# Two of the three ScalarE steps of a float64-to-float32 conversion write float32 words in place of bf16 half-words

## The chip, the cores and the metric
The kernel runs on one core of a Trainium2 chip (trn2). The metric is the device time of one launch in microseconds (us). TensorE (PE) does the matmuls, ScalarE (ACT) activations and copies, VectorE (DVE) and GpSimd (POOL) elementwise work, and SyncE (SP) issues most of the DMAs.

## The reference, cut to what matters
Attention with a soft cap (4 batches, 12 heads, 448 positions, 64 per head) is followed by two mixers: a token mix and a channel MLP, then a Fourier mix, a normalization and a second channel MLP:

```python
scores = cap * np.tanh(scores / cap)          # attention, softmax over the last axis
h  = np.maximum(xt @ w_tok1, 0.0) @ w_tok2    # first mixer: tokens 448 -> 256 -> 448
h2 = np.maximum(u @ w_ch1, 0.0) @ w_ch2       # channels 768 -> 1536 -> 768
mixed = np.real(np.fft.fft(np.fft.fft(x, axis=1), axis=2))
ch = np.maximum(un @ w_ch1, 0.0) @ w_ch2      # second mixer: 768 -> 3072 -> 768
```

The factors 1/sqrt(n) make the weights of both mixers float64. They lie in device memory as 8-byte words, and the kernel turns them into float32 itself: this conversion is what the change touches.

## The kernel before, in words
**Stages.** In the trace the heads and the token mixing fill about the first 300 us. Then comes the first channel MLP (to about 600 us), then the Fourier mix for one pair of batches beside the MLP (600 to 750), the second channel MLP for one half (750 to 1050) and for the other, in seven products after Strassen, up to the end at 1469 us. Each float32 product is made as three matmuls of a high and a low part (`mm3`, lines 301 to 304).

**Conversion.** `convert` (line 351) turns a piece of up to 128 rows by 768 float64 values into float32. A DMA on SP's queue loads the piece with its first three bytes cut off (lines 364 to 368), so that each value fills two 32-bit words of the `raw` tile: word 0 holds bytes 3 to 6, and the lowest byte of word 1 holds byte 7, with sign and upper exponent. The other three bytes of word 1 hold the three lowest bytes of the next value, which nothing uses. Three ScalarE instructions (line 330, called in lines 370 to 373) turn byte 7 into the sign and the top of the exponent of a float32: the first reads int8, the second and third read what the one before wrote, and the third writes word 1 as int32. A DVE instruction (line 374) shifts word 0 and joins both into the result, either in place or in a tile `y`. Every operand of these steps steps by 8 bytes from value to value.

**Who calls it.** `tok_first` and `tok_second` convert four narrow pieces; `piece` (line 398) converts a piece that is needed soon, and splits it into high and low parts `wh`, `wl`; `ahead` (line 1271) converts weights of the second MLP early, and puts them back into device memory (`put`, line 415) from the tile `y`. For its first eight pieces it also splits and puts both parts.

**Order.** The order on every engine is fixed when the kernel is built. A planner (`Plan.run`) picks operations by ready time, cost and due-time offsets. A copy on ScalarE is charged `fixed["A"] + n / 1150` us, whatever types it reads and writes (line 321), and the DMA of a piece cols/350 us. The engines run their queues in that order; at run time only semaphores hold them. There are two `raw` tiles, and a third from the end of the heads on, and two `y` tiles.

Of the kernel before, what the change touches and what calls it, by code (L numbers as in the profile page):

```python
# [9 lines left out]
F32 = mybir.dt.float32  # L10
# [4 lines left out]
BF16 = mybir.dt.bfloat16  # L15
# [249 lines left out]
def kernel(  # L265
# [48 lines left out]
    def v(n):  # L314
        return {"V": fixed["V"] + n / 960}
# [13 lines left out]
    def copy(n, out, src, reads, writes, func=AF.Copy, **kw):  # L329
        pl.op(a(n), lambda e: A.activation(out=out(), in_=src(), func=func, **kw), reads, writes)  # L330
# [14 lines left out]
    def raw_slot():  # L345
        return pl.slot("raw", lambda sp: (sp or raw_p).tile([128, TW, 2], I32, tag="raw", name="raw"))

    def flat(raw, dt=I32):
        return raw().rearrange("p a b -> p (a b)").bitcast(dt)

    def convert(src, rows, cols, x=None):
        raw = raw_slot()
        top = (raw, "top")

        def word(i):
            return raw()[:rows, :cols, i]

        def part(dt, n):
            return lambda: raw().bitcast(dt)[:rows, :cols, n]

        def value(dt=F32):
            return x().bitcast(dt)[:rows, :cols] if x else flat(raw, dt)[:rows, :cols]

        pl.op(
            {"SP": cols / 350}, lambda e: nc.sync.dma_start(
                out=flat(raw, I8)[:rows, :8 * cols - 3], in_=src.bitcast(I8)[:, 3:]
            ), [], [raw], lag=2.15,
        )
        step = part(BF16, 2)
        copy(cols, step, part(I8, 4), [raw], [top], AF.Relu, bias=72.0)  # L370
        copy(cols, step, step, [raw], [top], AF.Prelu, scale=-1.0, bias=16.0, alpha=KINK)
        copy(cols, lambda: word(1), step, [raw], [top], AF.Prelu,
             scale=-FIELD / KINK, bias=-112.0 * FIELD, alpha=KINK)
        pl.op(v(cols), lambda e: V.scalar_tensor_tensor(
            out=value(I32), in0=word(0), scalar=5, in1=word(1), op0=ALU.logical_shift_right, op1=ALU.bitwise_or,
        ), [raw, top], [x or raw])
        return value, x or raw
# [20 lines left out]
    def piece(src, x=None, k=None, engs=vp):  # L398
        w, ws = w_slot()
        value, key = convert(src, 128, DM, x)  # L400
        halves(DM, value, part(w, 0), part(w, 1), [key, w], ws[1:], engs)
        if k is not None:
            put(value, [key], k)
        return w, ws
# [42 lines left out]
    def phase_ab(heads, mixer, banks_a, banks_b):  # L447
# [29 lines left out]
        def tok_first():  # L477
            for i in range(2):
                value, key = convert(tok1[i], CP, 2 * DTOK)
                split_in(2 * DTOK, value, key, lambda i=i: rows2(w1h, i), lambda i=i: rows2(w1l, i), "w1", i)  # L480

        def tok_second():
            for i in range(2):
                value, key = convert(tok2[i], 128, S)
                split_in(S, value, key, lambda i=i: w2h[:, i, :], lambda i=i: w2l[:, i, :], "w2", i)
# [1470 lines left out]
```

## Time and profile before

| | us |
|---|---|
| median of 3 runs | 1470.07 (1463.83 to 1480.21) |
| the profiled execution | 1470.81 |
| its span, first to last instruction | 1469.0 |
| PE busy | 1377.9 |
| DVE busy | 1035.2 |
| ACT busy | 912.1 |
| POOL busy | 307.4 |

The busy time of an engine is the sum over its instructions. The chain of waits follows the last instruction back to what released it, step by step. The mean granted TensorE clock was 0.976 of full speed.

### The profile page before, as it was taken

Reading aid. Unit: us, or ns where it says so; the run is one execution under the profiler, and the core shown is the slowest. Engines: PE = TensorE matmul, PEld = TensorE weight load, DVE = VectorE, ACT = ScalarE, POOL = GpSimd, SP = SyncE. Lnnn points to the kernel's source line nnn. Section 1 sums busy time; section 2 is a strip of 40 time slices with the busy share of each in tenths; the row PEclk is TensorE's granted clock in tenths of the full one; section 3 lists DMA queues with packets and bytes.
Section 4 is the critical chain, followed back from the end, with each engine's and each line's share of the span. In section 5 each row is a group of like instructions: output and inputs, shape, how many; then the busy total and the mean of one; then the engine's idle time right before and its main releaser. Section 6 shows DMA issues by size and latency. Waiting matters only on the chain.

```text
span 1469.0 us, 18918 instructions
## 1 busy us (share of the span) xinstructions
PE 1377.9 (94%) x7398; PEld 1134.4 (77%) x7398; DVE 1035.2 (70%) x1076; ACT 912.1 (62%) x899; POOL 307.4 (21%) x166
## 2 busy tenths in 40 slices
PE   7899999989989879999998999889989999999997
PEld 2345545589879769899987889878778998999986
DVE  7887888646543445566886888575888778767698
ACT  8977897689899998212329552767722454444542
POOL 3332314100000000000000445221233223222341
PEclk9999999999999989999999999999999999999998
DMA  4222121027767776622436869886729866633332
GB/s 125 80 66 95 55 85 57 8 86 240 262 217 226 218 244 216 188 87 99 149 113 225 277 242 346 306 306 223 244 90 326 303 228 220 228 109 108 99 118 97
DMA packets 83771, 257.53 MB, mean 175 GB/s; under 512 B 9376, under 2 KB 12320, under 8 KB 83682
## 3 DMA queue, kind: packets, MB, share of 16 engines
q1 hardware_dynamic: 82528, 253.70, 52.0%
q0 software_dynamic: 1152, 2.62, 0.7%
q8 instruction: 58, 0.95, 0.3%
q14 instruction: 31, 0.25, 0.0%
q10 hardware_dynamic: 2, 0.00, 0.0%
HBM read 181.47 MB, written 74.81 MB: 174 GB/s over the span
## 4 chain that ended last, share of the span: by engine, by line
PE 58%; ACT 20%; DMA 10%; DVE 7%; issue 4%; SPq 1%; POOL 0%; DVEq 0%; ACTq 0%; POOLq 0%
PE mm L302 15%; PE mm L303 15%; PE mm L304 15%; ACT raw L330 13%; PE sc L519 3%; PE av L587 3%; DMA kept<-raw 3%; DMA raw<-in_m_dram 2%; ACT t L524 2%; ACT t L544 2%; PE mx L714 2%; DMA kept<-y 1%; PE av L603 1%; DMA wl<-kept 1%; DMA raw<-kept 1%
## 5 line engine op out<-in xcount | busy, mean ns | idle before, releaser
L330 ACT ACTIVATE raw<-raw 128x768 bf16<-128x768 int8 (+6 forms) x251 | 372.7, 1509 | 65.3 <-DMA raw<-kept 34.1
L302 PE MATMUL mm<-u,wh 128*128 128x448 f32 x804 | 296.9, 369 | 15.1 <-ACT wh L330 6.7
L303 PE MATMUL mm<-u,wh 128*128 128x448 f32 x828 | 304.6, 368 | 1.8 <-DVE u L333 1.8
L304 PE MATMUL mm<-u,wl 128*128 128x448 f32 x804 | 295.8, 368 | 0.0
L302 PE MATMUL mm<-r,wh 128*128 128x448 f32 x618 | 234.2, 379 | 26.3 <-DVE z L333 12.2
L303 PE MATMUL mm<-r,wh 128*128 128x448 f32 x624 | 235.1, 377 | 10.4 <-DVE r L333 4.8
L333 DVE TENSOR_TENSOR z<-mm,z 128x896 f32<-128x896 f32 (+1 forms) x205 | 203.6, 1011 | 49.3 <-PE mm L304 48.3
L304 PE MATMUL mm<-r,wl 128*128 128x448 f32 x618 | 231.0, 374 | 0.0
L330 ACT ACTIVATE wh<-wl 128x768 fp32r<-128x768 f32 x113 | 95.6, 848 | 163.7 <-DMA wl<-kept 159.7
L302 PEld LDWEIGHTS mm<-u,wh 128*128 128x128 f32 x804 | 152.4, 190 | 30.8 <-ACT wh L330 7.0
L303 PEld LDWEIGHTS mm<-u,wh 128*128 128x128 f32 x828 | 156.7, 189 | 15.1 <-DVE u L333 2.6
L333 POOL TENSOR_TENSOR wl<-wl,wh 128x768 fp32r<-128x768 f32 x37 | 75.1, 2034 | 426.9 <-ACT wh L330 218.3
L304 PEld LDWEIGHTS mm<-u,wl 128*128 128x128 f32 x804 | 152.4, 190 | 13.5 <-DVE wl L333 0.5
L302 PEld LDWEIGHTS mm<-r,wh 128*128 128x128 f32 x618 | 120.1, 194 | 43.6 <-DVE z L333 11.7
L303 PEld LDWEIGHTS mm<-r,wh 128*128 128x128 f32 x624 | 121.4, 195 | 22.9 <-DVE r L1524 5.7
L536 POOL PARTITION_ALL_REDUCE mb<-m x48 | 90.8, 1939 | 182.5 <-DVE m L333 153.4
L304 PEld LDWEIGHTS mm<-r,wl 128*128 128x128 f32 x618 | 119.9, 194 | 10.3
L333 DVE TENSOR_TENSOR wl<-wl,wh 128x768 fp32r<-128x768 f32 x76 | 83.8, 1108 | 50.9 <-ACT wh L330 50.7
L330 ACT ACTIVATE u<-u 128x896 fp32r<-128x896 f32 (+4 forms) x61 | 53.8, 892 | 105.5 <-DVE u L333 78.2
L330 ACT ACTIVATE r<-mm 128x896 fp32r<-128x896 f32 (+5 forms) x81 | 66.9, 831 | 75.9 <-PE mm L304 37.0
L333 DVE TENSOR_TENSOR t<-t,mb 112x1792 f32<-112x1792 f32 x48 | 103.4, 2176 | 6.3 <-POOL mb L536 6.3
L524 ACT ACTIVATE t<-sc,scl 112x896 f32<-112x896 f32 x96 | 92.8, 1012 | 9.0 <-PE sc L519 8.4
(191 smaller groups left out, 2139.7 us busy)
## 6 DMA issues: line engine op xcount, KB each, us to landing
wl<-kept SPq DMA_DIRECT2D x133, 384.0 KB, 3.7
raw<-in_m_dram SPq DMA_DIRECT2D x48, 767.6 KB, 5.0
raw<-kept SPq DMA_DIRECT2D x71, 384.0 KB, 4.6
kept<-raw SPq DMA_DIRECT2D x68, 384.0 KB, 4.8
raw<-in_c_dram SPq DMA_DIRECT2D x24, 767.6 KB, 5.0
kept<-y SPq DMA_DIRECT2D x44, 384.0 KB, 4.0
u<-kept SPq DMA_DIRECT2D x24, 448.0 KB, 6.1
qr<-in_qk_dram SPq DMA_DIRECT2D x23, 448.0 KB, 3.3
```

What stands on the lines that cost most here:

```text
L302: T.matmul(out=dst, lhsT=wh, rhs=xh, start=first, stop=False, skip_group_check=more)
L303: T.matmul(out=dst, lhsT=wh, rhs=xl, start=False, stop=False, skip_group_check=more)
L304: T.matmul(out=dst, lhsT=wl, rhs=xh, start=False, stop=last, skip_group_check=more)
L330: pl.op(a(n), lambda e: A.activation(out=out(), in_=src(), func=func, **kw), reads, writes)
L333: pl.op(engs, lambda e: eng[e].tensor_tensor(out=out(), in0=in0(), in1=in1(), op=op), reads, writes)
L519: T.matmul(out=ps()[:CP, k, :S], lhsT=qr()[d, S + c * CP:S + (c + 1) * CP], rhs=qr()[d, :S], start=True, stop=True)
L524: pl.op(a(W2, 0.06), lambda e, c=c, ps=ps: A.activation(out=tl()[:, c], in_=ps()[:CP, :, :S], func=AF.Tanh, scale=scl[:CP, 0:1]), [ps, tl] ...
L536: pl.op({"P": 1.9}, lambda e, k=k: P.partition_all_reduce(mb()[:, k], mx()[:, k], CP, bass_isa.ReduceOp.max), [mx, mb], [kb], hold=0.75)
L544: pl.op(a(2 * W2, 0.1), lambda e, k=k: A.activation(out=tl()[:, :, k], in_=tl()[:, :, k], func=AF.Exp, scale=cap_sb[:CP, 0:1]), [tl], [ke])
L587: T.matmul(out=ps()[d, :S], lhsT=vv()[:, c, d], rhs=tl()[:, c, hd], start=(c == 0), stop=(c == NCH - 1))
L603: T.matmul(out=ps()[32 * k:32 * k + 32, :S], lhsT=ones[:CP, 0:32].bitcast(F32), rhs=tl()[:, c, hd], start=(c == 0), stop=(c == NCH - 1))
L714: T.matmul(out=ps()[:, :S], lhsT=channels_of(rt()[:, tb, c], kc % NJ), rhs=wt[:, tb, :], start=False, stop=last, skip_group_check=True)
```

## The change
The first and the second ScalarE step of the conversion write, and the second and third read, a float32 in word 1 in place of a bf16 in its lower half. The functions, scales and biases stay, and so do the operations, their number, their tiles and what they are charged in the plan.

```diff
@@ -366,7 +366,7 @@
                 out=flat(raw, I8)[:rows, :8 * cols - 3], in_=src.bitcast(I8)[:, 3:]
             ), [], [raw], lag=2.15,
         )
-        step = part(BF16, 2)
+        step = part(F32, 1)
         copy(cols, step, part(I8, 4), [raw], [top], AF.Relu, bias=72.0)
         copy(cols, step, step, [raw], [top], AF.Prelu, scale=-1.0, bias=16.0, alpha=KINK)
         copy(cols, lambda: word(1), step, [raw], [top], AF.Prelu,
```

`part(BF16, 2)` is half-word 2 of each group of 8 bytes, `part(F32, 1)` is word 1, and `word(1)` is the same place as int32.

## Rows read from the trace of the kernel before

**Rows 1.** Profile page, busy time of each engine, and its share in 40 slices.

```profile
PE 1377.9 (94%) x7398; PEld 1134.4 (77%) x7398; DVE 1035.2 (70%) x1076; ACT 912.1 (62%) x899; POOL 307.4 (21%) x166
ACT  8977897689899998212329552767722454444542
```

**Rows 2.** Windows by stage: from:to, length, busy (instructions), granted clock, DMA share, GB/s.

```profile
0.00:300.00 300.00, 283.57 (x2038) 139.84 (x2039) 236.73 (x223) 244.17 (x259) 92.48 (x55) 0.99 0.25 76
300.00:390.00 90.00, 83.25 (x409) 76.71 (x409) 48.98 (x50) 78.45 (x71) 1.20 (x1) 0.96 0.51 175
390.00:550.00 160.00, 136.21 (x627) 121.69 (x626) 73.28 (x75) 156.89 (x113) 1.85 (x1) 0.94 0.72 230
550.00:600.00 50.00, 49.69 (x238) 45.49 (x237) 25.61 (x27) 38.74 (x30) 4.35 (x5) 0.97 0.65 221
600.00:750.00 150.00, 148.61 (x803) 137.03 (x802) 105.22 (x140) 34.52 (x43) 2.13 (x4) 1.00 0.37 118
750.00:850.00 100.00, 89.71 (x486) 80.32 (x484) 77.45 (x93) 64.73 (x60) 17.44 (x8) 0.97 0.66 228
850.00:1000.00 150.00, 141.06 (x660) 128.31 (x661) 112.64 (x124) 78.33 (x76) 52.57 (x29) 0.95 0.85 295
1000.00:1050.00 50.00, 47.71 (x231) 42.70 (x230) 28.20 (x32) 45.34 (x49) 8.45 (x6) 1.00 0.72 234
1300.00:1350.00 50.00, 50.00 (x248) 46.23 (x247) 33.53 (x33) 22.94 (x27) 14.57 (x7) 1.00 0.36 106
```

**Rows 3.** Chain of waits by line, 390 to 550 us.

```profile
by line: ACT raw L330 71.2%; issue 11.6%; ACT wh L330 4.1%; DMA raw<-in_m_dram 3.9%; ACT r L330 3.0%; PE mm L303 1.4%; DVE r L787 1.3%; DVE raw L374 1.2%; DVE y L374 1.1%; PE mm L304 0.7%; PE mm L302 0.5%; SPq L416 0.2%; DVE wl L333 0.0%; A
```

**Rows 4.** Waits of PE, 390 to 550 us: total us, times, longest.

```profile
PE mm L302 <- ACT r L330: 8.9, 2, 5.3
PE mm L302 <- ACT wh L330: 6.7, 1, 6.7
```

**Rows 5.** ACT's instructions by form, whole span: count, busy us, mean ns, idle before.

```profile
L330 ACT ACTIVATE raw<-raw 128x768 bf16<-128x768 bf16 x72 | 140.5, 1951 | 1.6
L330 ACT ACTIVATE raw<-raw 128x768 bf16<-128x768 int8 x72 | 140.3, 1956 | 26.5 <-DMA raw<-in_m_dram 10.8 <-DMA raw<-in_c_dram 9.5 <-DMA kept<-raw 5.2
L330 ACT ACTIVATE wh<-wl 128x768 fp32r<-128x768 f32 x113 | 95.6, 848 | 163.7 <-DMA wl<-kept 159.7 <-DVE raw L333 3.2
L330 ACT ACTIVATE raw<-raw 128x768 int32<-128x768 bf16 x72 | 65.1, 904 | 1.6
L330 ACT ACTIVATE raw<-raw 112x512 bf16<-112x512 int8 x2 | 2.7, 1358 | 0.0
L330 ACT ACTIVATE raw<-raw 112x512 int32<-112x512 bf16 x2 | 1.4, 688 | 0.0
```

**Rows 6.** DVE's instructions by form, 390 to 550 us.

```profile
L374 DVE SCALAR_TENSOR_TENSOR y<-raw 128x768 int32<-128x768 int32 x21 | 20.7, 984 | 46.3 <-ACT raw L330 46.3
L333 DVE TENSOR_TENSOR wl<-raw,wh 128x768 fp32r<-128x768 f32 x9 | 8.6, 956 | 11.3 <-ACT wh L330 11.3
```

**Rows 7.** ACT's instructions by form, 390 to 550 us.

```profile
L330 ACT ACTIVATE raw<-raw 128x768 bf16<-128x768 int8 x31 | 60.4, 1950 | 1.0 <-DMA raw<-in_c_dram 0.9
L330 ACT ACTIVATE raw<-raw 128x768 bf16<-128x768 bf16 x31 | 60.1, 1940 | 0.8
```

**Rows 8.** DMA issues, 300 to 620 us: count, KB each, us to landing.

```profile
raw<-in_m_dram SPq DMA_DIRECT2D x27, 767.6 KB, 4.9
kept<-y SPq DMA_DIRECT2D x44, 384.0 KB, 4.0
```

**Rows 9.** Chain of waits by line, 300 to 390 us.

```profile
by line: DMA kept<-y 23.6%; ACT raw L330 19.7%; DMA raw<-in_m_dram 11.8%; PE mx L714 6.9%; PE mm L302 5.5%; PE mm L303 5.0%; PE mm L304 4.9%; DVE y L374 4.3%; DVE y L333 3.2%; issue 3.2%; ACT u L330 2.9%; PE mx L710 2.4%; ACT y L330 2.0%; A
```

**Rows 10.** Chain of waits by line, 765 to 830 us, then ACT's forms there.

```profile
by line: ACT raw L330 35.3%; PE mm L302 12.1%; PE mm L304 11.4%; PE mm L303 11.3%; issue 10.4%; DMA raw<-in_m_dram 6.5%; ACT r L330 4.6%; ACT u L330 2.9%; DVE z L333 1.7%; DVE raw L374 1.6%; DVE mm L791 1.6%; PE mm L907 0.9%; ACTq L330 0.1%
...
L330 ACT ACTIVATE raw<-raw 128x768 bf16<-128x768 bf16 x7 | 13.6, 1943 | 0.2
```

## The prediction, made before the changed kernel had run

> **What bounds the kernel now.** I began with the busy times: PE is busy for 94% of the span, ACT for 62%, which by itself would put ACT off the path. The slices say otherwise: ACT's digits stand at 9 in a run of slices in the first half and at 2 to 7 later [rows 1]. So I cut the span into stages. Between 390 and 550 us ACT is busy for 156.89 of 160 us, while PE runs only 627 matmuls; between 1300 and 1350 us, a stretch of nearly the same three-matmul products, PE runs 248 in 50 us at full clock, 0.2016 us each [rows 2]. At that rate the 627 need 126.4 us, so the stage is 33.6 us longer than PE needs. That includes PE's lower clock: the mean granted clock is 0.94 there against 1.00, that is, part of the time at 1.2 GHz in place of 2.4, in a stage in which PE stands waiting. The chain of waits runs through ACT's conversion steps for 71.2% of the stage [rows 3], and PE waits longest for other ACT results, evictions `r` and splits `wh`, that stand behind conversions in ACT's queue [rows 4]. Here ACT sets the time. Elsewhere PE does: 148.61 of 150 us from 600 to 750 us [rows 2].
>
> **The price of one step.** The second and third steps of the conversion read the same bf16 half-words at the same 8-byte distance. The second writes bf16 and takes 1951 ns, the third writes int32 words and takes 904 ns [rows 5]. The first reads int8, writes bf16 and takes 1956 ns. What the two slow ones share and the fast one lacks is the 2-byte output. A contiguous float32 copy of the same size takes 848 ns [rows 5], so 904 is near the floor. After the change the first two steps write 4-byte words where the third writes them now: I take 904 ns for both. Bounds: 848 below, 1956 above (if int8 reading, in the first, or float32 reading at 8 bytes' distance, in the second and third, costs as much as the half-word writes). No ACT row shows such a float32 read; on DVE, line 374 reads 4-byte words at 8 bytes' distance and takes 984 ns, against 956 for a contiguous operation of the same size [rows 6], so I price it at nothing, and put the upper end into a rival.
>
> The saving is 1047 + 1052 = 2099 ns for each 768-wide piece; the rows count 72, so 151 us of ACT's time. The two pieces of 512 columns have 1358 against 688 ns, the same pattern [rows 5].
>
> One page speaks against this. The Trainium skill (ScalarE: Activation LUTs, section What ACT_TABLE_LOAD costs) says an ACTIVATE runs at one element per cycle and lane for every function, float32 and bf16 alike; by its 186 + 0.833 N ns a step of 768 takes an estimated 826 ns whatever the type, and the change would save nothing. The trace disagrees on the steps of today by more than a factor of two.
>
> **Stage by stage.** The plan's costs don't see the type, so every queue keeps its order; no wait, DMA or instruction is added, and nothing is moved past anything. Only durations change, and what follows from them.
>
> *390 to 550 us.* 31 + 31 slow steps [rows 7] shorten by 1.05 us each: 65 us off ACT's 156.89, leaving 92, less than the 126.4 that PE needs. PE becomes the bound, and at most 33.6 us can come back. What is late next is the load of a piece: a `raw` tile is refilled only when the DVE step has released it, 4.9 us to landing [rows 8], then ACT 3 x 0.9, DVE 0.98, about 8.6 us; over three tiles 2.9 us per piece, where PE's need leaves 126.4/31 = 4.1. A `y` tile has 0.98 of DVE and a put of 4.0 us to landing [rows 8], 5 us over two tiles: 2.5. Both fit. But DMA's busy share of 0.72 over 160 us would become 0.91 over 126.4, and between 850 and 1000 us, at 0.85, PE runs 660 matmuls, 133 us of work in 150, so queues crowd there [rows 2]. I take 27 of the 33.6.
>
> *300 to 390 us.* The largest terms of the chain are `kept<-y` (23.6%) and loads (11.8%); ACT's conversions have 19.7% [rows 9]. The puts of the eight pieces that are put three times bound it, and don't get faster. PE is idle for 6.75 us [rows 2]; I take 4 (between 0 and 6.75).
>
> *550 to 600 us.* 238 matmuls need 48.0 of 50 us [rows 2]: 1 us.
>
> *0 to 300 us.* PE is idle for 16.4 us [rows 2], and the few conversions stand between tanh and exp in ACT's queue. I take 4 (0 to 16.4).
>
> *750 to 850 us.* The chain has 35.3% of 65 us in conversions, 23 us, and 7 pieces shorten by 14.7 us [rows 10]; PE is idle for 10.3 [rows 2]. The reductions of the Fourier mix go through DVE as well, so I take 8. *1000 to 1050 us*: ACT is busy for 45.34 us and PE idle for 2.3 [rows 2]; 2. *850 to 1000 us* and after 1050: nothing; DMA or PE sets the pace.
>
> A lead won before 600 us is kept: PE has no slack from 600 to 750 us to lose it in. Sum: 4 + 4 + 27 + 1 + 8 + 2 = 46 us. The profiled execution took 1470.81 us (its span 1469.0 and 1.8 around it), 0.7 from the median of 1470.07, so I forecast **1425 us**.
>
> **The rivals.**
> *DMA takes ACT's place.* If the stage from 390 to 550 us can't go above the share of 0.75 (a little over its 0.72 now), it shrinks only to 160 x 0.72 / 0.75 = 154 us: 6 in place of 27, and the total is 1446. For it: the loads wait for tiles, and faster steps make them come together. Against: 0.85 is held for 150 us at 295 GB/s later [rows 2].
>
> *More comes back.* Waits after 850 us also come from evictions behind late conversions. If all 33.6 come back, and of the 6.75, 16.4, 10.3 and 2.3 some 28, and 8 of the 17 us that 850 to 1000 us lacks, it is 70 us: 1400.
>
> *The type makes no difference.* By the page's rule, as a mechanism of this kernel: the 1951 and 1956 ns come from function or data (Relu and Prelu with a bias), not from output size, and the steps stay so: 1470. Against: the third step is also a Prelu with scale, bias and alpha, on the same bytes, at 904 [rows 5]. The Trainium skill's page on ScalarE, named above, is where this rule stands.
>
> *Slower.* Reading float32 at 8 bytes' distance is slow on ACT. The first step becomes 904, and the second and third take R each; today's three make 4.81 us, so it decides from R = 1.95 up. At R = 2.35 (1.95 and 0.4 more) a piece takes 5.6 us, 0.8 more, and 31 pieces on the ACT-bound chain, with the 7 at 765 us, add 30 us: 1500. Against: DVE's 984 [rows 6], and the third step's 904 for a read of the same pitch.
>
> **How the numbers follow.** Forecast and its surroundings (1410 to 1440) 0.70; DMA instead (1440 to 1456) 0.12; more (1395 to 1410) 0.11; no difference 0.04; slower 0.03. The range reaches from 1400 to 1446: the whole first case, and most of its two neighbours. About 1% (15 us) is what a measurement here can tell from no change; the runs spread by that much. Faster by over 1% (under 1455) needs only a third of the forecast gain: 0.91. Within 1%: the no-difference case and the tail of the DMA case, 0.06. Slower: 0.03.
>
> **What would show it.** In the changed trace: `raw<-raw` float32 steps at about 0.9 us, none near 1.95; ACT's total near 760 us; the chain between 390 and 510 us through PE, with conversions no more its largest term; DMA's share there above 0.8; PE's granted clock near 1.00. I am wrong in the price if either step stays above 1.5 us; wrong in the path if the steps take 0.9 us and the time is above 1446, and then the waits name the `raw` loads or the `kept<-y` puts.

## The result and the profile after

The changed kernel takes 1401.44 us (median of 4 runs, 1397.42 to 1406.28) against 1474.16 for the kernel before beside it: a ratio of 0.9515, 95% interval 0.9448 to 0.9582. In a second comparison the same kernel had 0.9548 (0.9509 to 0.9586). The forecast was 1425 with a range of 1400 to 1446, so the time lies 1.4 us inside the low edge: 73 us were won where the sum had 46.

The price of a step first. ACT's instructions by form, whole span, of the changed kernel (to hold against [rows 5]: count, busy us, mean ns, idle before):

```profile
L330 ACT ACTIVATE raw<-raw 128x768 f32<-128x768 f32 x72 | 65.7, 913 | 1.6
L330 ACT ACTIVATE raw<-raw 128x768 int32<-128x768 f32 x72 | 65.4, 908 | 1.6
L330 ACT ACTIVATE raw<-raw 128x768 f32<-128x768 int8 x72 | 65.0, 906 | 73.5 <-DMA raw<-in_m_dram 36.1 <-DMA raw<-in_c_dram 30.4 <-issue 3.6
```

1951 and 1956 ns became 913 and 906; the third step, 904 before, took 908. Then the page, and the last line as it was before:

```profile
PE 1352.8 (97%) x7398; PEld 1121.7 (80%) x7398; DVE 1037.7 (74%) x1076; ACT 769.4 (55%) x899; POOL 302.8 (22%) x166
...
ACT  8977897676687763123255513657313643444442
...
L330 ACT ACTIVATE raw<-raw 128x768 f32<-128x768 int8 (+6 forms) x251 | 221.3, 891 | 116.7 <-DMA raw<-kept 39.9
```

```profile
L330 ACT ACTIVATE raw<-raw 128x768 bf16<-128x768 int8 (+6 forms) x251 | 372.7, 1509 | 65.3 <-DMA raw<-kept 34.1
```

The run of nines in ACT's slices [rows 1] is gone. The group of ACT instructions from `raw` to `raw`, all conversions and 23 splits, has 221.3 us; before it had 372.7, so 151 us less, about what the price times the count said. ACT as a whole lost 142.7 us (912.1 to 769.4, where the prediction had near 760): busy time counts a stretch once where two instructions overlap, and with idle time between them fewer do.

Where the time came from is best read by cutting the changed trace where PE has issued as many matmuls as at 300, 390, 550, 600, 750, 850, 1000 and 1050 us before. Windows of the changed kernel, cut so (columns as in [rows 2]):

```profile
0.00:290.10 290.10, 279.70 (x2039) 139.51 (x2040) 237.32 (x223) 235.11 (x260) 92.69 (x55) 1.00 0.26 79
290.10:369.90 79.80, 79.80 (x409) 74.50 (x408) 47.64 (x49) 54.87 (x70) 1.16 (x1) 1.00 0.57 190
369.90:499.40 129.50, 127.80 (x626) 117.28 (x625) 73.58 (x76) 97.22 (x114) 1.85 (x1) 1.00 0.85 289
499.40:548.90 49.50, 49.50 (x237) 45.66 (x236) 25.69 (x27) 25.53 (x30) 4.33 (x5) 0.97 0.68 227
548.90:698.60 149.70, 148.72 (x803) 137.12 (x802) 105.10 (x140) 34.51 (x43) 2.13 (x4) 1.00 0.36 117
698.60:786.60 88.00, 84.82 (x486) 77.56 (x484) 76.94 (x93) 48.40 (x60) 16.62 (x8) 1.00 0.73 259
786.60:930.60 144.00, 137.57 (x662) 124.52 (x661) 115.05 (x123) 64.19 (x76) 50.29 (x29) 0.99 0.88 309
930.60:978.10 47.50, 47.11 (x231) 42.79 (x230) 29.94 (x32) 36.88 (x47) 8.38 (x5) 1.00 0.76 243
```

The matmul counts match those of [rows 2] within two, so the lengths can be subtracted; the last stage is what is left of the span, 1395.7 - 978.1 after and 1469 - 1050 before:

| stage of before (us) | before | after | won | forecast |
|---|---|---|---|---|
| 0 to 300 | 300 | 290.1 | 9.9 | 4 |
| 300 to 390 | 90 | 79.8 | 10.2 | 4 |
| 390 to 550 | 160 | 129.5 | 30.5 | 27 |
| 550 to 600 | 50 | 49.5 | 0.5 | 1 |
| 600 to 750 | 150 | 149.7 | 0.3 | 0 |
| 750 to 850 | 100 | 88.0 | 12.0 | 8 |
| 850 to 1000 | 150 | 144.0 | 6.0 | 0 |
| 1000 to 1050 | 50 | 47.5 | 2.5 | 2 |
| 1050 to 1469 | 419 | 417.6 | 1.4 | 0 |
| sum | 1469 | 1395.7 | 73.3 | 46 |

In the stage that ACT bound (now 369.9 to 499.4 us), PE is busy for 127.80 of 129.5 us at a clock of 1.00, where it had 0.94. What waits there now? ACT's waits in that stage (total us, times, longest):

```profile
ACT raw L330 <- DMA raw<-in_c_dram: 15.9, 10, 3.3
ACT raw L330 <- DMA raw<-in_m_dram: 11.8, 10, 2.6
```

and PE's, all of them, against the 15.6 us of its two largest in [rows 4]:

```profile
PE mm L302 <- ACT r L330: 0.8, 1, 0.8
PE mm L303 <- DVE r L787: 0.8, 1, 0.8
```

ACT now stands waiting for the loads, which is the wait that took the place of its work. The chain of waits of the stage goes through those loads:

```profile
by line: DMA raw<-in_m_dram 16.9%; PE mm L303 15.2%; PE mm L302 15.0%; PE mm L304 14.7%; DMA raw<-in_c_dram 13.2%; ACT raw L330 12.7%; issue 3.8%; DVE y L374 2.9%; ACT wh L330 1.7%; DVE z L333 1.6%; DVE r L787 0.8%; SPq L416 0.7%; DVE raw L
```

The conversions fell from 71.2% [rows 3] to 12.7%. The largest single line is now a load, and PE's three lines together have 44.9%. The chain's 30% of loads must not be taken for a price: beside them PE has 1.7 us of idle time in 129.5. A chain names one path; the busy time of the engine that must do the work says whether a shorter path would help.

### The profile page after: what moved, and what is told of

The parts are those of the page before. It is cut to its first block, busy times and chain, and to the rows that moved or that the text cites. A ratio compares the mean times of both kernels' runs of the same rounds, so it can differ in the third digit from the quotient of the medians.

```text
span 1395.7 us, 18918 instructions
## 1 busy us (share of the span) xinstructions
PE 1352.8 (97%) x7398; PEld 1121.7 (80%) x7398; DVE 1037.7 (74%) x1076; ACT 769.4 (55%) x899; POOL 302.8 (22%) x166
## 4 chain that ended last, share of the span: by engine, by line
PE 73%; DMA 12%; ACT 6%; DVE 6%; issue 2%; SPq 0%; POOL 0%; DVEq 0%; ACTq 0%; POOLq 0%
PE mm L302 18%; PE mm L303 18%; PE mm L304 18%; PE sc L519 4%; PE av L587 4%; DMA raw<-in_m_dram 3%; DMA wl<-kept 3%; PE av L603 2%; PE mx L714 2%; ACT raw L330 2%; DMA kept<-y 2%; ACT t L524 1%; ACT t L544 1%; DMA kept<-raw 1%; DMA raw<-in_c_dram 1%
## 5 line engine op out<-in xcount | busy, mean ns | idle before, releaser
L330 ACT ACTIVATE raw<-raw 128x768 f32<-128x768 int8 (+6 forms) x251 | 221.3, 891 | 116.7 <-DMA raw<-kept 39.9
L303 PE MATMUL mm<-r,wh 128*128 128x448 f32 x624 | 231.1, 370 | 10.2 <-DVE r L1524 5.0
L302 PE MATMUL mm<-r,wh 128*128 128x448 f32 x618 | 229.4, 371 | 3.2 <-DVE z L333 1.3
L304 PE MATMUL mm<-r,wl 128*128 128x448 f32 x618 | 227.8, 369 | 0.0
L303 PEld LDWEIGHTS mm<-r,wh 128*128 128x128 f32 x624 | 118.9, 191 | 22.0 <-DVE r L1524 6.0
L302 PEld LDWEIGHTS mm<-r,wh 128*128 128x128 f32 x618 | 117.4, 190 | 16.7 <-issue 3.4
```

The costliest lines, as they stand in the source:

```text
L302: T.matmul(out=dst, lhsT=wh, rhs=xh, start=first, stop=False, skip_group_check=more)
L303: T.matmul(out=dst, lhsT=wh, rhs=xl, start=False, stop=False, skip_group_check=more)
L304: T.matmul(out=dst, lhsT=wl, rhs=xh, start=False, stop=last, skip_group_check=more)
```

## The experiments

**One step at a time.** The first theory is that the 2-byte output is the price, whichever step writes it; the rivals put it on the int8 input or on the function.

```diff
-        step = part(F32, 1)
+        step, two = part(F32, 1), part(BF16, 2)
         copy(cols, step, part(I8, 4), [raw], [top], AF.Relu, bias=72.0)
-        copy(cols, step, step, [raw], [top], AF.Prelu, scale=-1.0, bias=16.0, alpha=KINK)
-        copy(cols, lambda: word(1), step, [raw], [top], AF.Prelu,
+        copy(cols, two, step, [raw], [top], AF.Prelu, scale=-1.0, bias=16.0, alpha=KINK)
+        copy(cols, lambda: word(1), two, [raw], [top], AF.Prelu,
```

> Only the first ScalarE step writes float32; the second reads it and still writes bf16. Theory (the 2-byte output at 8 bytes' distance is the price, whoever writes it): the first step takes 0.91 us, the second stays at 1.95. ACT in the stretch that was 390 to 550 us loses 31 x 1.05 = 33 us of 157 and comes to 124, about PE's need of 126, so the larger half of the gain comes already: some 45 of the 73 us, ratio to before 0.970. Rival 1 (the conversions lie on the path one for one): half the gain, 36 us, ratio 0.975. Rival 2 (int8 reading is what made the first step slow): the first step stays near 1.95 and the ratio is 1.00.

The second run of the pair is the same with the two types exchanged (`step, two = part(BF16, 2), part(F32, 1)`).

> Only the second ScalarE step writes float32; the first still writes bf16 from int8. Theory: the first stays at 1.95 us, the second takes 0.91, and the time is that of the run with only the first step changed, within 1%: ratio to before 0.970. Rival (the price depends on what is read or on the function, Relu from int8 against Prelu): one of the two halves gives clearly more than the other, as 0.96 against 0.99.

The first gave 1417.96 us, ratio 0.9650 (0.9607 to 0.9693), the second 1424.56 us, 0.9691 (0.9660 to 0.9722), against 1470.85 before. ACT's forms, first with only the first step changed, then with only the second:

```profile
L330 ACT ACTIVATE raw<-raw 128x768 bf16<-128x768 f32 x72 | 140.9, 1957 | 1.6
L330 ACT ACTIVATE raw<-raw 128x768 f32<-128x768 int8 x72 | 65.4, 912 | 38.0 <-DMA raw<-in_m_dram 18.2 <-DMA raw<-in_c_dram 13.7 <-DMA kept<-raw 2.2
L330 ACT ACTIVATE raw<-raw 128x768 int32<-128x768 bf16 x72 | 65.1, 904 | 1.6
```

```profile
L330 ACT ACTIVATE raw<-raw 128x768 bf16<-128x768 int8 x72 | 140.3, 1957 | 38.4 <-DMA raw<-in_m_dram 21.5 <-DMA raw<-in_c_dram 12.3 <-issue 4.3
L330 ACT ACTIVATE raw<-raw 128x768 f32<-128x768 bf16 x72 | 65.6, 911 | 1.6
L330 ACT ACTIVATE raw<-raw 128x768 int32<-128x768 f32 x72 | 65.4, 908 | 1.6
```

Every bf16 output takes 1957 ns, from int8 or from float32; every 4-byte output takes 904 to 912, from int8, bf16 or float32. In these steps input type and function play no part. One half of the change gives 53 or 46 us, where 45 were expected and half of the gain would be 36; the whole gives 70 to 73, less than the sum of the halves. Does the first step give more than the second? The intervals of the two ratios overlap, and up to the matmul that ended the stage at 1050 us before, the two traces win nearly the same, 52.9 and 54.4 us (it is reached at 997.1 and 995.6 us). The stage that ACT bound shows why the halves don't add up; its window with only the first step changed, cut by matmul count:

```profile
374.90:510.90 136.00, 128.63 (x626) 117.28 (x625) 73.46 (x76) 127.41 (x113) 1.85 (x1) 1.00 0.83 275
```

ACT has 127.41 us of work there and PE 126.4 by count: where both need about the same, the stage takes 136, some nine more than either. With only the second step changed it takes 136.0 as well, with 127.00 us of ACT's work.

**Where the late gain comes from.** Is the lead won after 750 us due to the late conversions, or to what the early ones left behind?

```diff
+    turns = []
...
-        step = part(F32, 1)
+        wide = []
+
+        def step():
+            if not wide:
+                wide.append(len(turns) < 56)
+                turns.append(1)
+            return part(F32, 1)() if wide[0] else part(BF16, 2)()
```

> The change for the first 56 conversions in the order of execution (all up to 600 us of the kernel before), bf16 as before for the 20 after 750 us. Theory (each stage's gain comes from its own conversions): the lead of 51 us at 600 us is there, and about 20 of the 22 us that the changed kernel wins after 750 us are lost: gain 53 us, ratio to before 0.964, ratio to the full change 1.014. Rival (the lead after 750 us is an after-effect of the earlier stages, whose puts land sooner): gain 65 to 73 us, ratio to before 0.951 to 0.956.

It took 1416.76 us, ratio 0.9651 (0.9614 to 0.9688): 54 us won, 53 expected; the after-effect would have given 65 or more. ACT's forms show 20 slow pieces left:

```profile
L330 ACT ACTIVATE raw<-raw 128x768 bf16<-128x768 int8 x20 | 39.1, 1953 | 14.0 <-DMA raw<-in_m_dram 8.7 <-issue 5.3
```

Its stages that were 750 to 850, 850 to 1000 and 1000 to 1050 us, cut by matmul count:

```profile
695.80:796.10 100.30, 89.17 (x486) 80.01 (x484) 77.54 (x94) 64.93 (x60) 17.23 (x8) 0.97 0.65 228
796.10:942.50 146.40, 138.91 (x660) 126.15 (x661) 113.62 (x123) 77.97 (x76) 51.95 (x29) 0.98 0.86 302
942.50:992.90 50.40, 47.70 (x231) 42.57 (x230) 28.91 (x33) 45.39 (x49) 8.47 (x6) 1.00 0.71 232
```

The lead of 54 us is there at the first of these cuts (750 - 695.8), and the first and the third of the stages are as long as before.

**How much ACT still holds.** The first two steps are dropped; the plan keeps its places, so that no queue changes order.

```diff
-        copy(cols, step, part(I8, 4), [raw], [top], AF.Relu, bias=72.0)
-        copy(cols, step, step, [raw], [top], AF.Prelu, scale=-1.0, bias=16.0, alpha=KINK)
-        copy(cols, lambda: word(1), step, [raw], [top], AF.Prelu,
-             scale=-FIELD / KINK, bias=-112.0 * FIELD, alpha=KINK)
+        for _ in range(2):
+            pl.op(a(cols), lambda e: None, [raw], [top])
+        copy(cols, lambda: word(1), part(I8, 4), [raw], [top], AF.Prelu,
+             scale=0.0, bias=0.0, alpha=KINK)
```

> The first two ScalarE steps are left out altogether, and the third writes zeros, so the weights' signs and upper exponents are missing; all other instructions, DMAs and their order stay. ACT loses another 76 x 1.8 = 135 us against the changed kernel. Theory (with the change ACT is off the path and PE sets the time between 300 and 600 us, with some 10 us lost to waits there): at most 10 to 15 us come back, 1387 to 1397 us, ratio to before 0.945. Rival 1 (ACT's conversions still set part of the time): 30 us or more, under 1372, ratio 0.93. Rival 2 (DMA has become the bound): no gain over the changed kernel, 1400, ratio 0.951.

1395.02 us, ratio 0.9493 (0.9461 to 0.9526): 6 us under the changed kernel's 1401.44 of an earlier comparison. Both were run again side by side.

> The changed kernel once more, beside the next one on the same chip: about 1400 us, ratio to before 0.9515.

> The kernel without the first two ScalarE steps once more, to hold it against the changed kernel on the same chip. Theory (ACT is off the path): 3 to 8 us less than the changed kernel, 0.2 to 0.6%. Rival (ACT's conversions still set part of the time): 15 us less or more.

1403.22 us, 0.9548 (0.9509 to 0.9586), against 1392.33 us, 0.9469 (0.9420 to 0.9519). The medians differ by 10.9 us, more than the theory's 3 to 8 and less than the rival's 15; the intervals overlap, so by the times the worth stays open between nothing and some 1%. The traces narrow it. The matmul that ended the stage at 1050 us before is reached at 978.1 and 974.8 us in two traces of the changed kernel, and at 974.3 and 970.6 in the two without the steps: some 4 us. What comes after it converts nothing and takes between 415.1 and 426.3 us in the nine traces of this case, so more than 4 us can't be put down to ACT. That is small beside the 127 us of ACT's busy time that went (769.4 to 642.5). In the stage that ACT bound, the window of the first of the two runs without the steps is

```profile
368.80:496.00 127.20, 127.20 (x627) 117.52 (x626) 73.76 (x76) 45.58 (x53) 1.86 (x1) 1.00 0.85 294
```

PE is busy for all of it. Over four kernels ACT's work in this stage goes 156.9, 127.4, 97.2, 45.6 us, and the stage takes 160, 136, 129.5, 127.2: it follows ACT as long as ACT needs more than PE's 127, and PE below. The last step, from 129.5 to 127.2, need not be ACT's. The kernel with only the early conversions changed has the same conversions in this stage as the changed kernel, and PE is busy for all of it too:

```profile
370.80:498.00 127.20, 127.20 (x627) 117.51 (x627) 73.69 (x75) 97.58 (x113) 1.87 (x1) 1.00 0.85 289
```

So with the change ACT no longer sets the time of this stage; what is left over 127.2 differs from one execution to the next.

**The price by itself.** Copies of eleven forms between two idle tiles, ahead of the first work. Each form is given as type, distance in bytes from value to value, and place, of the output and then of the input; `view` makes such an operand:

```diff
...
+        n = 448
+        for dst, src in (
+            ((F32, 8, 1), (F32, 8, 1)), ((F32, 8, 1), (BF16, 8, 2)), ((F32, 8, 1), (I8, 8, 4)),
+            ((BF16, 8, 2), (F32, 8, 1)), ((BF16, 8, 3), (F32, 8, 1)), ((BF16, 4, 0), (F32, 8, 1)),
+            ((BF16, 2, 0), (F32, 8, 1)), ((U16, 8, 2), (F32, 8, 1)), ((I8, 8, 4), (F32, 8, 1)),
+            ((F32, 4, 0), (F32, 4, 0)), ((F32, 4, 0), (BF16, 2, 0)),
+        ):
+            for _ in range(2):
+                A.activation(out=view(zb, *dst[:2], n, dst[2]), in_=view(za, *src[:2], n, src[2]), func=AF.Copy)
+            n -= 4
```

> The changed kernel with 22 ScalarE copies ahead of it, two of each form, between two tiles that hold nothing yet; each form has a width of its own, from 448 values down by 4, by which it is found in the trace. Outputs and inputs of 4, 2 and 1 bytes, at 8 bytes' distance, at 4 bytes' distance and contiguous. Theory 1 (a write of less than a 4-byte word is the price, and only where its neighbour in the word isn't written with it): 0.6 us for every float32 output, whatever is read; 1.2 us for bf16 and uint16 in either half of the word at 8 bytes' distance, for bf16 at 4 bytes' distance and for int8; 0.6 us for contiguous bf16. Theory 2 (any 2-byte output is slow on ScalarE): 1.2 us for contiguous bf16 too. Theory 3 (the overlap of output and input in one word is the price, as the conversion works in place): 0.6 us for all forms, since these copies go from tile to tile. The whole takes about 20 us longer than the changed kernel.

It took 1412.68 us (one run), about 10 more than the changed kernel, not 20. The width tells the forms apart: 448, 444 and 440 are float32 at 8 bytes' distance from float32, bf16 and int8; 436 and 432 bf16 in the lower and upper half of a word at 8; 428 bf16 at 4; 424 contiguous bf16; 420 uint16 and 416 int8 at 8; 412 and 408 contiguous float32 from float32 and bf16:

```profile
L1836 ACT ACTIVATE z<-z 128x432 bf16<-128x432 f32 x2 | 2.4, 1184 | 0.0
L1836 ACT ACTIVATE z<-z 128x436 bf16<-128x436 f32 x2 | 2.3, 1168 | 0.1
L1836 ACT ACTIVATE z<-z 128x420 uint16<-128x420 f32 x2 | 2.3, 1132 | 0.1
L1836 ACT ACTIVATE z<-z 128x416 int8<-128x416 f32 x2 | 2.2, 1122 | 0.1
L1836 ACT ACTIVATE z<-z 128x428 bf16<-128x428 f32 x2 | 1.4, 706 | 0.0
...
L1836 ACT ACTIVATE z<-z 128x448 f32<-128x448 f32 x2 | 1.2, 606 | 0.2
L1836 ACT ACTIVATE z<-z 128x440 f32<-128x440 int8 x2 | 1.2, 604 | 0.1
L1836 ACT ACTIVATE z<-z 128x444 f32<-128x444 bf16 x2 | 1.2, 604 | 0.1
L1836 ACT ACTIVATE z<-z 128x424 bf16<-128x424 f32 x2 | 1.2, 577 | 0.1
L1836 ACT ACTIVATE z<-z 128x412 f32<-128x412 f32 x2 | 1.1, 546 | 0.1
```

Ten of the eleven forms come out as the first theory had them: outputs of 1 or 2 bytes at 8 bytes' distance cost about twice a 4-byte one, also from tile to tile, so working in place is not the cause (theory 3 falls), and the 4-byte ones cost the same whatever is read. Contiguous bf16 costs no more than float32, so 2-byte outputs as such are not slow (theory 2 falls). But bf16 at 4 bytes' distance took 706 ns, not 1200: "a part of a word written alone" isn't the whole rule, and why the distance matters was not settled.

## Why the prediction was right, and where it was off

**The range: right by little.** The time is 1.4 us over the range's low end of 1400, less than the scatter of its own runs (1397.42 to 1406.28), so that the range held it is partly luck. The case that came true is the rival *more comes back* (1395 to 1410), which had a chance of 0.11, not the middle, which had 0.70. Of that rival's terms, all of the 33.6 us came to 30.5, the 28 us in four other stages to 34.6, and the 8 us from 850 to 1000 to 6.0.

**The price: right.** 904 ns was taken for both steps; 906 and 913 were measured. The reasoning, that the two slow steps share the 2-byte output and the fast one lacks it, held for these steps. As a rule it was too wide: a contiguous 2-byte output is not slow (577 ns for 424 values), only one that leaves a distance. The rival that the type makes no difference fell with the first row. The Trainium skill (ScalarE: Activation LUTs, section What ACT_TABLE_LOAD costs) gives one element per cycle for float32 and bf16 alike: the runs agree for functions (Relu 906 ns, Prelu 913), for inputs and for contiguous outputs (577 ns for 424 bf16 values, 546 for 412 float32), and disagree for bf16 outputs at 8 bytes' distance, 1168 for 436.

**The slower rival: wrong.** Float32 read at 8 bytes' distance costs ACT no more than bf16 did: 908 ns in the third step, where bf16 took 904.

**The ACT-bound stage: right.** PE's need was worked out by count and rate as 126.4 us; the stage took 129.5 with the change, 127.2 without the two steps. I kept back 6.6 of the 33.6 us for DMA; 3.1 were lost, and 0.8 and 2.2 in two other traces with the same conversions there (127.2 and 128.6 us). ACT's work fell to 97.2 us and not to 92, as its busy time counts overlaps once; PE's need stayed the larger all the same.

**DMA in ACT's place: wrong.** The share rose to 0.85 at 289 GB/s, above the 0.75 at which that rival capped it. The loads did become slower, as the DMA issues of the changed kernel from 290 to 560 us show (count, KB, us to landing; [rows 8] had 4.9 and 4.0):

```profile
raw<-in_m_dram SPq DMA_DIRECT2D x27, 767.6 KB, 5.9
kept<-y SPq DMA_DIRECT2D x44, 384.0 KB, 5.3
```

ACT waits for them, PE doesn't.

**The other stages: sized too small by 23.5 us** (0 to 300: 9.9 for 4; 300 to 390: 10.2 for 4; 750 to 850: 12.0 for 8; 850 to 1000: 6.0 for 0; after 1050: 1.4 for 0). The main step that failed is the ceiling I set by PE's idle time. From 300 to 390 us I wrote "between 0 and 6.75", and 10.2 came back, since PE's busy time itself fell from 83.25 to 79.80 for the same 409 matmuls: a granted clock of 0.96 against 1.00 is lost time that counts as busy. Idle time and 0.04 of 90 us together are 10.4. From 750 to 850 us the same holds in part: idle 10.3, won 12.0, busy 89.71 to 84.82; the clock's 0.97 against 1.00 is 3 us of that fall of 4.9, and no run settles the rest. In that stage I also shared the gain with DVE without a row that said so.

In the stage from 300 to 390 us the path was wrong too. I let the puts bound it, as the chain's largest term. But PE's idle time before was ended by other work:

```profile
PE mx L710 <- ACT z L330: 4.1, 1, 4.1
PE mm L302 <- DVE z L333: 2.6, 1, 2.6
```

With the change PE waits for nothing in this stage, though the puts have become slower (5.3 us in place of 4.0).

From 0 to 300 us ACT's busy time fell by 9.1 us (244.17 to 235.11) and the stage by 9.9, so nearly all of ACT's saving came back; I had taken 4 of a possible 16.4.

From 850 to 1000 us I took the stage for DMA's because the share was 0.85, though seven pieces are converted there; it now runs at 0.88 and 309 GB/s. The kernel with only the early conversions changed tells the parts. Its stages from 750 us on take 100.3, 146.4 and 50.4 us: all of the 12.0 and the 2.5 us are the late conversions' own. Of the 6.0 they would have 2.4, and 3.6 would come from the lead before, but that split is not shown: it is from one execution each, and two more traces with all conversions changed (the second comparison and the copies ahead) have 141.9 and 141.3 us in this stage where the first had 144.0.

The stage after 1050 us has no conversions. By spans less the same cut it took 419.0 before, 417.6 after, and 415.1 (1408.0 - 992.9) with only the early conversions changed, so its 1.4 us can't be told from scatter.

## What to carry to other kernels

Compare instructions that differ in one thing: three steps over the same bytes, one of them twice as fast, price an edit of types before anything runs. To find what a stage can give back, don't stop at idle time, which leaves out what a lower clock costs. Where a stage has the same matmuls as one that runs full, multiply their count by that stage's rate: 126.4 us from 390 to 550, and 127.2 was reached. Where it has others, as from 750 to 850 us (486 at this rate would be 98 of 100 us, and 12 came back), add to the idle time the stage's length times what the granted clock lacks: 10.3 and 3 us there. And when two engines need about the same time in a stage, more than either may be needed: half of this change took ACT to PE's 127 us, and the stage still took 136.

## What the runs showed of the hardware that was not expected

ScalarE's outputs of 1 or 2 bytes at 8 bytes' distance take twice the time of 4-byte outputs at the same distance (1957 against 904 to 913 ns for 768 values), in either half of the word, and for uint16 and int8 as for bf16; at 4 bytes' distance bf16 takes 706 ns for 428 values, between the two. The Trainium skill (SBUF — State Buffer, section Door 1: The DMA port swizzle) says that a pattern may step for free as long as accesses share a 16-byte line, up to 8 values of bf16; for ScalarE's writes the runs disagree already at a step of 2 and of 4 bf16 values. Reads agree: bf16 and int8 at 8 bytes' distance cost no more than float32 (604 ns for 444 and 440 values).
